# The first key tile's ten matmuls: wide part of all five slices first, the narrow part with the gate column behind them

## The chip, the cores and the metric

One core of a Trainium2 chip runs the whole kernel as one program. The metric is device time in microseconds (us).

## The reference, cut to what matters

```
g = sigmoid((x * gate_w).sum(-1, keepdims=True))     # one number for each token
a = linear attention of x (q, k, v from x @ wqkv; 32 heads of 20) @ wo
b = a two-layer mixer block on x (layernorm, w1, shift, w2, layernorm, w3, w4)
return g * a + (1 - g) * b
```

x is 2048 tokens x 640, in bfloat16. The kernel gets the gate's dot product almost for free: `gate_w` is one more column beside the 640 key columns, so the key matmul of a token tile yields 640 key columns, two columns of ones (a row sum for the layernorm) and the gate column, 643 in all. The kernel gives a matmul at most 512 columns, so a slice of the contraction (128 of 640 rows, five slices) takes a wide matmul of 512 columns and a narrow one of 131, and the gate column is in the narrow one.

## The kernel before

A scheduler of the kernel's own orders the work for each engine. Each operation lists what it reads and writes, and it waits for the last writer of everything in its lists. The loads that matter come from one queue, in this order:

```python
dma_in(x_tok[:, 0, :], ...); dma_in(x_tok[:, 1, :], ...)     # two x tiles
load_wq(0)                                                   # query weights, slice 0
dma_in(x_tok[:, 2:4, :], ...)
for k in range(1, KD):
    load_wq(k)
for k in range(KD):
    dma_in(wkg[:, k, 0:D], A_wqkv[128 * k:128 * (k + 1), D:2 * D], "wk%d" % k)     # key weights
dma_in(wkg[:, :, D + 2:D + 3], gate_w.rearrange("(k p o) -> p k o", p=128, o=1), "gw", noncontig=True)
for c in range(1, NCH):
    dma_in(x_tok[:, 4 * c:4 * c + 4, :], ...)                # 640 KB each
    ...                                                      # transposes of these x tiles
```

TensorE first runs some needless matmuls to warm up, then four query tiles with their slices mixed in the order in which weights arrive (`q_four`, 40 matmuls), then the first key tile. Both the query tiles and the first key tile go through `stream`, which makes one operation of a wide and a narrow matmul:

```python
def stream(order, w, n2, done):
    ...
        def fn(e, l=l, b=b, k=k):
            e.matmul(ps[:, b, 0:512], l, w[:, k, 0:512], start=(k == 0), stop=(k == KD - 1))
            return e.matmul(ps[:, b + 1, 0:n2], l, w[:, k, 512:512 + n2], start=(k == 0), stop=(k == KD - 1))
        pe(fn, [w[:, k, 0:512 + n2], l], [ps[:, b, 0:512], ps[:, b + 1, 0:n2]], cost=272.0)
        ...

def k_first():
    stream([(0, k) for k in range(KD)], wkg, 131, k_out)
```

Because the operation's read list is `w[:, k, 0:512 + n2]`, even its wide matmul stands behind the load of the gate column. Later key tiles (`k_tile`) run five wide and then five narrow matmuls, each group as one operation.

Of the kernel before, what the change touches and what calls it, by code (L numbers as in the profile page):

```python
# [11 lines left out]
D = 640  # L12
# [5 lines left out]
KD = D // 128  # L18
# [398 lines left out]
def _build(nc, A_x, A_wqkv, A_wo, B_w1, B_w2, B_w3, B_w4, gate_w, out, dbg=None, stop=None):  # L417
# [42 lines left out]
    ps = nc.alloc_psum_tensor("ps", [128, 8, 512], F32)  # L460
# [33 lines left out]
    xT = ra.alloc("xT", [128, KD, S], BF16)  # L494
    GT = ra.alias("GT", [128, KD, D], BF16, ra.last_addr, KD * S * 2)
    wkg = ra.alloc("wkg", [128, KD, NK], BF16)
# [34 lines left out]
    def pair():  # L531
        best = None
        for k_ in range(4):
            q_ = (bank_rr[0] // 2 + k_) % 4
            tf = 0.0
            ok = True
            for b in (2 * q_, 2 * q_ + 1):
                if b in bank_pend or b in bank_hold:
                    ok = False
                lk = sch.locks.get(b)  # L540
                if lk is not None:
                    tf = max(tf, sch.ev_time.get((lk[1].sem, lk[1].val), 1e18))
            if ok and (best is None or tf < best[0]):
                best = (tf, 2 * q_)
        b = best[1]
        bank_rr[0] = b + 2
        bank_pend.update((b, b + 1))
        return b
# [36 lines left out]
    def pe(fn, reads, writes, cost=500.0):  # L585
        for w_ in writes:
            sp_, rl = sch.rects(w_)
            if sp_ == "ps":
                for (_p0, _p1, lo, hi) in rl:
                    for b in range(lo // PS_BANK, (hi - 1) // PS_BANK + 1):  # L590
                        bank_pend.discard(b)
        return sch.op("pe", fn, reads, writes, cost=cost)
# [50 lines left out]
    def activation(out_ap, in_ap, func, scale=1.0, bias=0.0, accum=None):  # L643
        rd = [in_ap] + [a for a in (scale, bias) if not isinstance(a, (int, float))]
        wr = [out_ap] + ([accum] if accum is not None else [])
        n = nfree(out_ap)
        cost = max(150.0, 100.0 + 0.833 * n + (70.0 if in_psum(in_ap) else 0.0)) + 45.0 * (len(rd) - 1)
        if accum is not None:
            cost += 91.0
        st_ = ACT_SET.get(func)  # L650
        if st_ is not None and st_ != sch.act_func:
            cost += 1290.0
            sch.act_func = st_
        if accum is not None:
            return act(lambda e: e.activation(out_ap, in_ap, func, bias=bias, scale=scale, accum_out=accum), rd, wr, cost=cost)  # L655
        return act(lambda e: e.activation(out_ap, in_ap, func, bias=bias, scale=scale), rd, wr, cost=cost)  # L656
# [96 lines left out]
    def t_x(t):  # L753
        b = bank()
        tr_group(b, [x_tok[:, t, 128 * k:128 * (k + 1)] for k in range(KD)])
        src = psb(b, 0, D).rearrange("p (k c) -> p k c", k=KD)
        dst = xT[:, :, 128 * t:128 * (t + 1)]
        copy(dve, dst, src)

    def phi(b, dst, after_exp=None):  # L760
        se = slot("E", 3)
        src = psf[:, 512 * b:512 * b + D]
        activation(Er[:, se, :], src, ACTF.Exp)
        if after_exp is not None:
            after_exp()
        ts(dve, Er[:, se, :], Er[:, se, :], 1.0, EPS_PHI, ALU.min, ALU.add)
        return stt(dst, src, 1.0 + EPS_PHI, Er[:, se, :], ALU.add, ALU.max)
# [72 lines left out]
    def warmup(cols, cyc):  # L840
        b = bank()
        steps = [512] * (cols // 512) + [128] * (cols % 512 // 128)

        def fn(e):
            ins = None
            for n in steps:
                ins = e.matmul(ps[:, b, 0:n], xn[:, 0, 0:128], xn[:, 0, 0:128].unsqueeze(1).to_broadcast([128, n // 128, 128]), start=True, stop=True)  # L847
            return ins
        pe(fn, [xn[:, 0, 0:128]], [ps[:, b, :]], cost=cols * cyc)
# [8 lines left out]
    def stream(order, w, n2, done):  # L858
        bs = {}
        for t, k in order:  # L860
            if k is None:
                if t is None:
                    warmup(256, 0.42)
                else:
                    t_x(t)
                continue
            if k == 0:
                bs[t] = pair()
                bank_hold.update((bs[t], bs[t] + 1))
            b = bs[t]  # L870
            l = xT[:, k, 128 * t:128 * (t + 1)]
# [5 lines that stand above are left out]
            if k == KD - 1:  # L877
                bank_hold.difference_update((b, b + 1))
                done(t, b)
# [6 lines left out]
    def k_out(t, b):  # L886
        k_done[t] = phi(b, pk_tok[:, t, :], lambda: activation(lr[:, t, :], ps[:, b + 1, 129:131], ACTF.Copy))
        activation(junk[:, 0, :], x_tok[:, t, :], ACTF.Square, accum=st1[:, 1, t:t + 1])

    def k_first():  # L890
        stream([(0, k) for k in range(KD)], wkg, 131, k_out)

    def addA(name, dur, fn, deps=()):
        IT.add("A", name, dur, fn, deps)
# [4 lines left out]
    addA(("warm", 1), 0.0, lambda: warmup(WARM2, 0.42))  # L899
    addA(("q", 3), 5.44, q_four)  # L900
    addA(("k", 0), 1.36, k_first)
    for i in range(1, 4):
        addA(("k", i), 1.36, lambda t=i: k_tile(t))
# [409 lines left out]
```

## Time and profile before

| | before |
|---|---|
| median of the first three runs | 260.96 us (260.87 to 261.06) |
| span of the profiled execution | 259.6 us |
| TensorE busy | 255.7 us, 99% |
| last query matmul starts | 11.31 us |
| gate column lands | 11.71 us |
| first key matmul starts | 11.80 us |

The page of the profiled execution: span, busy time by engine (of it the share of the span, and instructions), and the chain of work that ended last.

```profile
span 259.6 us, 4300 instructions
...
PE 255.7 (99%) x1690; PEld 132.2 (51%) x1690; DVE 151.7 (58%) x287; ACT 106.8 (41%) x216; POOL 92.8 (36%) x152
...
PE 97%; DMA 1%; DVE 0%; SPq 0%; issue 0%
```

TensorE (PE) is the bound: it works nearly all the time, and the chain is 97% PE. Only time in which it waits, or does needless work, can be won without taking work away. The list of waits of PE (who waited for whom, us in total, times, longest) is short:

```profile
PE ps L847 <- POOL xn L659: 1.1, 1, 1.1
PE ps L874 <- DMA wq<-in_A_wqkv_dram: 0.5, 1, 0.5
PE ps L874 <- issue: 0.3, 1, 0.3
```

The first is the start of the kernel, the second the wait for the first query weights, and the third is the first key tile. The timeline of PE there (start, duration, engine, line, operation, output and inputs, form):

```profile
11.10 0.38 PE L874 MATMUL ps<-wq,xT 128*128 128x512 bf16 x1
11.31 0.22 PE L875 MATMUL ps<-wq,xT 128*128 128x128 bf16 x1
11.80 0.38 PE L874 MATMUL ps<-wkg,xT 128*128 128x512 bf16 x1 [0.27 <-issue]
12.01 0.22 PE L875 MATMUL ps<-wkg,xT 128*128 128x131 bf16 x1
12.07 0.38 PE L874 MATMUL ps<-wkg,xT 128*128 128x512 bf16 x1
```

Read the starts, not the durations: a matmul's recorded end lies well past the start of the next one. A wide matmul follows a narrow one after 0.06 us (12.01 to 12.07), but the first key matmul follows the last query matmul after 0.49 us. So 0.43 us are lost, where the idle time in brackets says 0.27. The DMA issue table of a window around 6.9 us shows which load is late (the last key slice, then the gate column; the last number is us from issue to landing):

```profile
wkg<-in_A_wqkv_dram SPq DMA_DIRECT2D x1, 160.0 KB, 4.1
wkg<-in_gate_w_dram SPq DMA_DIRECT2D x1, 1.2 KB, 4.7
```

The gate column is issued at 6.96 us and lands at 11.71; the key slice before it landed at 10.63. (Landings to a hundredth are the semaphore updates in the trace; the table rounds.) The first key matmul starts 0.09 us after the gate column's landing. (The trace holds 640 packets of 2 bytes, one for each element of `gate_w`, moved between 9.09 and 11.38 us.)

### The profile page before, as it was taken

To read this page: it belongs to the slowest core of one execution; us is meant where nothing else is said; L and a number is where in the kernel's file an instruction comes from. 1 tells how busy PE (TensorE), PEld (TensorE's weight loads), DVE (VectorE), ACT (ScalarE), POOL (GpSimd) and SP (SyncE) were. 2 spreads that over 40 slices of the span, in tenths; PEclk is the share of its full clock that TensorE was granted. 3 is DMA by queue.
4 is the path that set the end of the run, shared out by engine and by line. 5 is a ranking of instruction groups with operands and counts; after the bars stand their busy time and mean duration, and the time that the engine had idled before them with its cause. 6 is when DMAs were issued, how large, how long until landed. Compare 5 with 4: busy or idle time off the path is not lost.

```text
span 259.6 us, 4300 instructions
## 1 busy us (share of the span) xinstructions
PE 255.7 (99%) x1690; PEld 132.2 (51%) x1690; DVE 151.7 (58%) x287; ACT 106.8 (41%) x216; POOL 92.8 (36%) x152
## 2 busy tenths in 40 slices
PE   7999999999999999999999999999999999999996
PEld 4555555554445454554444545554455544456453
DVE  1587887899902799999998407993033410143233
ACT  1496677751355766685854240005500045200000
POOL 4003995969863019667903202230011110021001
PEclk9999999999999999999999999999999999999999
DMA  6845969572656991752726650232000020000211
GB/s 195 260 104 146 198 176 143 167 139 44 110 108 123 352 337 36 72 101 52 105 56 124 124 61 0 41 85 78 0 3 0 3 101 0 0 3 1 104 51 51
DMA packets 51348, 24.99 MB, mean 96 GB/s; under 512 B 42708, under 2 KB 49917, under 8 KB 51328
## 3 DMA queue, kind: packets, MB, share of 16 engines
q1 hardware_dynamic: 49952, 21.31, 35.2%
q0 software_dynamic: 1136, 3.28, 5.8%
q8 instruction: 13, 0.21, 0.4%
q10 hardware_dynamic: 240, 0.13, 0.2%
q14 instruction: 7, 0.06, 0.1%
HBM read 12.05 MB, written 2.62 MB: 57 GB/s over the span
## 4 chain that ended last, share of the span: by engine, by line
PE 97%; DMA 1%; DVE 0%; SPq 0%; issue 0%
PE ps L600 61%; PE ps L1152 22%; PE ps L782 8%; PE ps L874 2%; DMA wq<-in_A_wqkv_dram 1%; PE ps L1064 1%; PE ps L1134 1%; PE ps L875 1%; DVE x_tok L639 0%; PE ps L954 0%; PE ps L983 0%; SPq L285 0%; PE ps L611 0%; PE ps L1131 0%; PE ps L847 0%
## 5 line engine op out<-in xcount | busy, mean ns | idle before, releaser
L600 PE MATMUL ps<-xnT,w 128*128 128x512 bf16 x360 | 81.5, 379 | 0.0
L1152 PE MATMUL ps<-w,h2T 128*128 128x512 bf16 (+1 forms) x416 | 58.8, 299 | 0.0
L656 ACT ACTIVATE h2T<-ps 128x512 bf16<-128x512 f32 x52 | 30.5, 598 | 67.5 <-PE ps L600 67.5
L600 PEld LDWEIGHTS ps<-xnT,w 128*128 128x128 bf16 x360 | 34.2, 98 | 38.5 <-issue 0.9
L639 DVE SCALAR_TENSOR_TENSOR x_tok<-ps,stg,abx 128x512 bf16<-128x512 f32 (+1 forms) x32 | 17.3, 550 | 61.5 <-PE ps L1152 61.5
L622 POOL TENSOR_SCALAR abx<-x_tok,stg 128x640 f32<-128x640 bf16 x16 | 14.8, 927 | 99.9 <-DVE x_tok L639 94.9
L1152 PEld LDWEIGHTS ps<-w,h2T 128*128 128x128 bf16 x416 | 32.2, 98 | 24.9 <-issue 1.1
L622 POOL TENSOR_SCALAR xn<-x_tok,st 128x640 bf16<-128x640 bf16 x32 | 34.4, 1082 | 14.3 <-DMA xnT<-xn 13.6
L656 ACT ACTIVATE Er<-ps 128x640 bf16<-128x640 f32 x32 | 22.5, 705 | 17.9 <-PE ps L600 8.5
L655 ACT ACTIVATE junk<-x_tok 128x640 bf16<-128x640 bf16 x32 | 23.6, 737 | 3.1 <-DVE x_tok L637 2.6
L600 PE MATMUL ps<-M_sb,pqnT 128*128 128x512 bf16 (+1 forms) x160 | 24.3, 299 | 0.0
L656 ACT ACTIVATE hsT<-ps 128x512 bf16<-128x512 f32 (+1 forms) x32 | 18.9, 594 | 13.0 <-PE ps L600 12.6
L600 PE MATMUL ps<-w,hsT 128*128 128x512 bf16 (+1 forms) x160 | 23.7, 299 | 0.0
L600 PE MATMUL ps<-wkg,xT 128*128 128x512 bf16 (+1 forms) x150 | 22.6, 299 | 0.0
L639 DVE SCALAR_TENSOR_TENSOR abx<-ps,stg,abx 128x640 f32<-128x640 f32 x16 | 14.1, 884 | 12.7 <-PE ps L600 11.7
L600 PEld LDWEIGHTS ps<-w,hsT 128*128 128x128 bf16 x160 | 13.3, 98 | 12.2
L600 PEld LDWEIGHTS ps<-M_sb,pqnT 128*128 128x128 bf16 x160 | 13.2, 98 | 10.9
L600 PE MATMUL ps<-wq,xT 128*128 128x512 bf16 (+1 forms) x120 | 18.3, 299 | 0.0
L782 PE MATMUL ps<-pk_tok,x_tok 128*128 128x512 bf16 x80 | 17.8, 379 | 0.0
L622 DVE TENSOR_SCALAR Er<-Er 128x640 bf16<-128x640 bf16 x32 | 11.6, 363 | 9.6 <-ACT Er L656 9.2
L637 DVE SCALAR_TENSOR_TENSOR x_tok<-ps,x_tok 128x640 bf16<-128x640 f32 x16 | 13.1, 820 | 6.4 <-PE ps L600 5.9
L600 PEld LDWEIGHTS ps<-wkg,xT 128*128 128x128 bf16 x150 | 12.2, 98 | 9.0
(75 smaller groups left out, 231.2 us busy)
## 6 DMA issues: line engine op xcount, KB each, us to landing
w<-in_B_w_dram SPq DMA_DIRECT2D x1, 2160.0 KB, 9.6
w<-in_B_w_dram SPq DMA_DIRECT2D x1, 2080.0 KB, 15.2
x_tok<-in_A_x_dram SPq DMA_DIRECT2D x3, 640.0 KB, 5.9
out_dram<-x_tok SPq DMA_DIRECT2D x3, 640.0 KB, 3.1
w<-in_B_w_dram POOLq DMA_DIRECT2D x8, 160.0 KB, 4.5
wq<-in_A_wqkv_dram SPq DMA_DIRECT2D x5, 160.0 KB, 3.6
wkg<-in_A_wqkv_dram SPq DMA_DIRECT2D x5, 160.0 KB, 4.3
wv<-in_A_wqkv_dram POOLq DMA_DIRECT2D x1, 800.0 KB, 5.9
```

The lines of the kernel that those rows point to most:

```text
L600: ins = e.matmul(out_ap, l, r, start=(i == 0), stop=(i == n - 1))
L622: return engf(lambda e: e.tensor_scalar(out_ap, in_ap, s1, s2, op0, op1), rd, [out_ap], cost=cost)
L637: return dve(lambda e: e.scalar_tensor_tensor(out_ap, in0, scalar, in1, op0, op1, accum_out=accum), rd, [out_ap, accum], cost=cost + 70.0)
L639: return dve(lambda e: e.scalar_tensor_tensor(out_ap, in0, scalar, in1, op0, op1), rd, [out_ap], cost=cost)
L655: return act(lambda e: e.activation(out_ap, in_ap, func, bias=bias, scale=scale, accum_out=accum), rd, wr, cost=cost)
L656: return act(lambda e: e.activation(out_ap, in_ap, func, bias=bias, scale=scale), rd, wr, cost=cost)
L782: ins = e.matmul(o, l, r, start=(t0 + q_ == 0), stop=(t0 + q_ == NT - 1))
L874: e.matmul(ps[:, b, 0:512], l, w[:, k, 0:512], start=(k == 0), stop=(k == KD - 1))
L875: return e.matmul(ps[:, b + 1, 0:n2], l, w[:, k, 512:512 + n2], start=(k == 0), stop=(k == KD - 1))
L1064: ins = e.matmul(o, l, r, start=st, stop=sp)
L1134: ins = e.matmul(ps[:, bm, :], l, w4[rows, KFF, 0:512], start=True, stop=False)
L1152: ins = e.matmul(o, l, r, start=False, stop=(i == KFF - 1), skip_group_check=(n0 > 0))
```

## The change

It takes the wide matmuls of the first key tile out of the gate column's wait: each matmul becomes an operation that lists only its own columns, and the five wide ones come first.

```diff
     def k_first():
-        stream([(0, k) for k in range(KD)], wkg, 131, k_out)
+        b = pair()
+        for n0, n1 in ((0, 512), (512, D + 3)):
+            o = ps[:, b + n0 // 512, 0:n1 - n0]
+            for k in range(KD):
+                l, r = xT[:, k, 0:128], wkg[:, k, n0:n1]
+                pe(lambda e, o=o, l=l, r=r, k=k: e.matmul(o, l, r, start=(k == 0), stop=(k == KD - 1)), [l, r], [o],
+                   cost=(n1 - n0) * 0.4167 + 2.5)
+        k_out(0, b)
```

## The prediction

> **What bounds the kernel now.** TensorE. The page's busy table gives PE 255.7 of 259.6 us (99%), and the chain that ended last is 97% PE. The list of waits names only three waits of PE: 1.1 us for the first memset, 0.5 us for the first query weights, and 0.3 us at the first key tile, marked "issue".
>
> **The first key tile.** In the timeline the last query matmul (128 wide) starts at 11.31 us and the first key matmul at 11.80, while elsewhere in that stage a wide matmul starts 0.05 to 0.06 us after a narrow one. So PE loses 0.49 - 0.06 = 0.43 us there (the profile shows 0.27 us of idle, as a matmul's modelled end lies past the next one's start).
>
> What ends the wait: the key weights' five loads land by about 10.6 us (in the DMA issue table, 4.1 to 4.3 us each), but the gate column, 1.2 KB, is issued at 6.96 and needs 4.7 us: it lands at about 11.7, just before the PE goes on. "DMA: Bandwidth & Descriptors" in the Trainium skill (section "Rules for kernel authors") says a non-contiguous last dimension is lowered to one descriptor per element; 4.7 us for 1.2 KB, the longest of this tile's six loads, agrees. Each slice's operation reads wide and narrow columns together, so even the first wide matmul waits for the gate column, which only the narrow part uses.
>
> **What the change does.** The same ten matmuls, five wide then five narrow; nothing removed. The wide ones no longer wait for the gate column. Their other inputs are ready: weights at 10.6 us, the PSUM pair when the DVE ends query tile 0 at 11.04 (10.22 + 0.82). Five wide ones take 5 x 0.216 = 1.08 us, so the narrow part begins at about 12.45, some 0.7 us after the gate column lands: the wait vanishes. Later key tiles have this very order and take 1.36 us per ten (20 in 2.73 us in the chain), the same as five pairs at 0.27. Semaphore increments go from 5 to 10; I expect nothing from that.
>
> **How much is critical.** All of it, if what follows keeps up. The matmuls run without a visible gap from 11.80 us to the end, so all shift by 0.43 us. Nearest dangers: DVE is busy without a break from 10.2 to 16.7 us, so PSUM pairs come free at unchanged times; but the second key tile's is free at 12.13 and wanted at 12.73, the third's at 13.23 against 14.1. The first transposed x tile of the next chunk lands at about 15.9, needed at 16.84. Later handoffs hang on PE's own progress. The instruction order is made by a list scheduler from modelled costs; this tile's moves by some 5 ns, so I expect the same order.
>
> **Predicted time.** 260.96 - 0.43 = 260.53 us, 8 in 10 between 260.25 and 260.9. Chances: faster by over 2% 0.5%, within 2% 98.5%, slower by over 2% 1%.
>
> **What would show each step.** First key matmul at about 11.37; no PE wait there in the list of waits; wide starts 0.216 apart; first narrow one at about 12.45; second key tile at about 12.73 instead of 13.17; exponential of key tile 0 at about 12.94 instead of 13.37; every later stage 0.43 us earlier; span about 259.2.
>
> **What would make it wrong.** The gate column landing at another time in unprofiled runs (earlier: less gain); a reordering by the scheduler later on; a fixed-time DMA that turns the lead into a new wait; noise of 0.2 us (the three runs span 260.87 to 261.06), about half the effect.

## The result, and the profile after

| first comparison, six runs each | before | changed |
|---|---|---|
| median | 260.91 us (260.47 to 261.39) | 260.60 us (260.43 to 261.00) |
| span of the profiled execution | 259.6 us | 259.5 us |

The ratio is 0.9989, with a 95% interval of 0.9976 to 1.0002. A ratio here is the mean time of one kernel's fast runs over the mean of the other's fast runs of the same rounds, so it is not quite the ratio of the medians. The time lies in the predicted range, 0.07 us from the predicted value. But the interval includes 1, and the profile does not show 0.43 us: the span fell by 0.1 us. The page of the changed kernel:

```profile
span 259.5 us, 4269 instructions
...
PE 254.6 (98%) x1659; PEld 133.0 (51%) x1690; DVE 151.7 (58%) x287; ACT 106.7 (41%) x216; POOL 92.8 (36%) x152
...
PE 95%; DVE 2%; issue 1%; ACT 0%; POOL 0%; POOLq 0%
```

PE seems 1.1 us less busy, but its count is 1659 where there are 1690 weight loads: 31 matmul records are missing from this trace. That is not the change's doing, as later traces of the kernel before lack some too. The list of waits of PE:

```profile
PE ps L847 <- POOL xn L659: 1.1, 1, 1.1
PE ps L600 <- issue: 0.2, 1, 0.2
PE ps L1159 <- issue: 0.2, 1, 0.2
```

The wait at the first key tile is gone. The two new lines of 0.2 us are holes left by missing records: counted from the start of the second key tile, the trace of the kernel before has a matmul at each of these two places, and this trace has none. The 2% of DVE in the chain comes from such a hole too, at 16.06 us, from which the chain was followed into DVE. The timeline of PE at the first key tile:

```profile
11.48 0.38 PE L874 MATMUL ps<-wq,xT 128*128 128x512 bf16 x1
11.69 0.22 PE L875 MATMUL ps<-wq,xT 128*128 128x128 bf16 x1
11.75 1.53 PE L896 MATMUL ps<-wkg,xT 128*128 128x512 bf16 x10
13.11 0.38 PE L600 MATMUL ps<-wkg,xT 128*128 128x512 bf16 x1
```

The first key matmul now follows the last query matmul after 0.06 us, and the ten take 1.37 us, as before (by the unrounded starts 1.366 and 1.373). The mechanism works as predicted. But the last query matmul starts at 11.69 us and not at 11.31. The query stage, which the change does not touch, ended 0.38 us later in this execution. The first half of that stage in the timeline of the kernel before:

```profile
3.69 0.75 PE L611 MATMUL ps<-ident,x_tok 128*128 128x128 bf16 x10
...
5.06 0.39 PE L874 MATMUL ps<-wq,xT 128*128 128x512 bf16 x1 [0.51 <-DMA wq<-in_A_wqkv_dram]
...
5.46 0.38 PE L874 MATMUL ps<-wq,xT 128*128 128x512 bf16 x1
...
6.48 0.38 PE L874 MATMUL ps<-wq,xT 128*128 128x512 bf16 x1
```

and of the changed kernel:

```profile
3.69 1.27 PE L611 MATMUL ps<-ident,x_tok 128*128 128x128 bf16 x10
...
5.11 0.58 PE L874 MATMUL ps<-wq,xT 128*128 128x512 bf16 x1
...
5.81 0.60 PE L874 MATMUL ps<-wq,xT 128*128 128x512 bf16 x1
...
6.86 0.38 PE L874 MATMUL ps<-wq,xT 128*128 128x512 bf16 x1
```

The same instructions take longer: ten transposes 1.27 us and not 0.75, a wide matmul 0.58 to 0.60 and not 0.38, until about 6.2 us. TensorE still ran at a slow starting clock there, about half of the later one (the transposes start 0.107 us apart and not 0.056), while in the first trace it had sped up by 3.7 us (its file records full clock from 3.74 us on; the changed kernel's file has no record of the clock). The Trainium skill, "TensorE: Matmul & The Clock Gate", part "The HAM clock gate (the "warmup" mystery)", says that full clock is granted after about 3.4 us of activity measured in a free-running window, so the moment varies from run to run. That the moment varies these traces show, with a spread of more than 2 us. The 3.4 us they do not show: in the first trace full clock came 2.7 us after the first matmul (1.05 to 3.74 us).

### The profile page after: what moved, and what is told of

It reads as the page before. It is cut to its first block, busy times and chain, and to the rows that moved or that the text cites. A ratio compares the mean times of both kernels' runs of the same rounds, so it can differ in the third digit from the quotient of the medians.

```text
span 259.5 us, 4269 instructions
## 1 busy us (share of the span) xinstructions
PE 254.6 (98%) x1659; PEld 133.0 (51%) x1690; DVE 151.7 (58%) x287; ACT 106.7 (41%) x216; POOL 92.8 (36%) x152
## 4 chain that ended last, share of the span: by engine, by line
PE 95%; DVE 2%; issue 1%; ACT 0%; POOL 0%; POOLq 0%
PE ps L600 60%; PE ps L1159 21%; PE ps L782 8%; PE ps L847 1%; DVE pq_tok L639 1%; PE ps L874 1%; PE ps L1071 1%; PE ps L1141 1%; DVE Er L622 1%; PE ps L611 1%; DVE x_tok L639 0%; PE ps L961 0%; PE ps L990 0%; PE ps L875 0%; ACT Er L656 0%
## 5 line engine op out<-in xcount | busy, mean ns | idle before, releaser
L600 PE MATMUL ps<-xnT,w 128*128 128x512 bf16 x349 | 80.4, 379 | 0.6 <-issue 0.2
L600 PE MATMUL ps<-M_sb,pqnT 128*128 128x128 bf16 (+1 forms) x156 | 23.6, 297 | 0.3
```

What stands on the lines that cost most here:

```text
L600: ins = e.matmul(out_ap, l, r, start=(i == 0), stop=(i == n - 1))
```

## The experiments

The model that I tested, called A2 in the expectations, is this:

- In the kernel before, the first key matmul starts at the later of two times: the end of the query stage (last query start + 0.055 us) and the gate column's landing + 0.09 us.
- In the changed kernel, it starts at the end of the query stage.
- All that follows takes a fixed time.

The last point was read from the traces: the span less the start of the second key tile is 246.41 or 246.42 us in every trace but two (the two are told of below). So the change is worth the wait in the execution at hand, and nothing where there is none. The rivals are B (no effect, all chance) and B' (wide-then-narrow order is itself cheaper than pairs).

In all kernels below the scheduler made the same order of work as in the kernel before, and all gave correct results. "Before" is the kernel before, run on the same chip: 260.87 us for the first four, 260.86 for the next four, 260.76 for the last four.

### The changed kernel again

Edit: none.

> The changed kernel again, unedited, to narrow the interval. Theory A (the change takes away the wait for the gate column's landing): 0.2 to 0.45 us faster than before, ratio about 0.9987, the first key matmul starts 0.06 us after the last query matmul. Theory B (the change does nothing, the difference of 0.3 us so far is noise of the start): ratio 1.0000 within 0.0005.

Measured: 260.86 us, ratio 1.0003 (0.9991 to 1.0015). In its trace the last query matmul starts at 11.74 us and the first key matmul at 11.79, 0.05 us later; the gate column had landed at 11.57. So the old order would not have waited in this execution (11.57 + 0.09 is before 11.79). The size expected by A is missed, and B's ratio is met. The timeline of PE and the gate column's line of the DMA issue table (window around 6.9 us):

```profile
11.74 0.22 PE L875 MATMUL ps<-wq,xT 128*128 128x128 bf16 x1
11.79 1.53 PE L896 MATMUL ps<-wkg,xT 128*128 128x512 bf16 x10
wkg<-in_gate_w_dram SPq DMA_DIRECT2D x1, 1.2 KB, 4.6
```

In this one execution there was nothing to remove.

### The gate column's load earlier

```diff
+    dma_in(wkg[:, :, D + 2:D + 3], gate_w..., "gw", noncontig=True)
     for k in range(KD):
         dma_in(wkg[:, k, 0:D], ..., "wk%d" % k)
-    dma_in(wkg[:, :, D + 2:D + 3], gate_w..., "gw", noncontig=True)
```

> The kernel before, its matmul order untouched, with the gate column's load issued ahead of the five key loads and not behind them. Theory A (wait for the gate column): the column lands at about 9 us, before the last query matmul, the first key pair starts 0.06 us after it, and the time falls as in the changed kernel, 0.2 to 0.45 us; the key loads land 0.5 us later each, still in time. Theory B' (wide-then-narrow order itself is cheaper than pairs on TensorE): no gain, as the pairs stay.

Measured: 261.07 us, ratio 1.0008 (0.9996 to 1.0020). The column landed at 8.88 us, and the first key pair started 0.05 us after the last query matmul, so the wait was gone with pairs as well. But that query stage ended late too (last start 11.78), because the first query weights landed at 5.50 us, 0.48 later than in the first trace of before. The expected gain is missed. An execution that would not have waited gains nothing from a column that comes earlier.

### The order without the release

```diff
-    ..., [l, r], [o], cost=...)
+    ..., [l, wkg[:, k, 0:D + 3]], [o], cost=...)
```

> The changed order, five wide and then five narrow, but each wide matmul declared to read the gate column too, so that the first one waits for it as before. Theory A: same time as before within 0.1 us, the first key matmul starts about 0.09 us after the gate column lands. Theory B' (the order is what is cheaper): as fast as the changed kernel, 0.2 to 0.45 us under before.

Measured: 260.89 us against 260.87 by medians; the ratio of 1.0022 (0.9993 to 1.0051) is drawn up by two runs over 262 us. The timeline of PE:

```profile
11.48 0.22 PE L875 MATMUL ps<-wq,xT 128*128 128x128 bf16 x1
11.65 1.53 PE L896 MATMUL ps<-wkg,xT 128*128 128x512 bf16 x10
```

The first key matmul starts 0.17 us after the last query matmul and 0.09 us after the gate column's landing at 11.56, so it waited 0.12 us though it stood in the new order. The ten take 1.36 us (the second key tile starts at 13.01), within 0.02 us of the pairs. That speaks against B': the order is worth nothing in itself; it only lets the wide matmuls go ahead.

### Pairs with separate waits

```diff
+        b = pair()
+        for k in range(KD):
+            for n0, n1 in ((0, 512), (512, D + 3)):
+                ...one operation for each matmul, with the read list of its own columns
```

> Pairs kept, wide then narrow for each slice, but each matmul is an operation of its own with its own waits, so only the first narrow matmul waits for the gate column. Theory A: one wide matmul, 0.216 us, is hidden in the wait; gain 0.2 us at most, about half of the change's, and the remaining wait stands between the first wide and the first narrow matmul. Theory B' (order): no gain. A theory that ten semaphore updates in place of five cost time would show as slower than theory A by the cost.

Measured: 260.63 us, ratio 0.9995 (0.9983 to 1.0007): no gain clear of noise. In its trace the last query matmul starts at 11.54, the first wide key matmul at 11.59, the first narrow one at 11.81, and the gate column lands at 11.66. The wait would have been 0.16 us (11.66 + 0.09 - 11.59), and one wide matmul of 0.216 us covers it. Ten operations took 1.38 us (11.59 to 12.97), so ten semaphore updates in place of five cost at most 0.02 us.

### The wait made long: the gate column's load behind 640 KB of x

```diff
-    dma_in(wkg[:, :, D + 2:D + 3], gate_w..., "gw", noncontig=True)
     for c in range(1, NCH):
         dma_in(x_tok[:, 4 * c:4 * c + 4, :], ..., "xc%d" % c)
+        if c == 1:
+            dma_in(wkg[:, :, D + 2:D + 3], gate_w..., "gw", noncontig=True)
```

In the kernel before (sent twice, as no chip ran it the first time; so with the three after it):

> The kernel before with the gate column's load issued one place later, behind the 640 KB load of x. Theory A2 (before: the key tile starts at the later of query end and gate landing plus 0.09 us; change: at query end; all that follows takes 246.4 us): the column lands at about 13.4 to 14 us, the key tile starts 0.09 us after it, and the time rises by 1.6 to 2.2 us over before. Theory B (noise): the traces so far are chance and the load's place does not matter: no change.

In the changed kernel:

> The changed kernel with the gate column's load behind the 640 KB load of x. Theory A2: the five wide matmuls, 1.08 us, run inside the wait, the first narrow one starts 0.09 us after the landing; so 1.08 us faster than the same delay in the kernel before, and 0.5 to 1.1 us slower than the kernel before without the delay. Theory B' (order is what matters) and B (noise): the same as the delayed kernel before within 0.3 us.

Measured: 262.66 us (ratio 1.0075, 1.0053 to 1.0097) and 261.49 us (1.0019, 1.0004 to 1.0035). Both agree with A2, and this pair is clear of noise: the intervals of the two do not touch, and the medians are 1.17 us apart. The timeline of PE in the kernel before with the late load:

```profile
11.54 0.22 PE L876 MATMUL ps<-wq,xT 128*128 128x128 bf16 x1
13.68 0.38 PE L875 MATMUL ps<-wkg,xT 128*128 128x512 bf16 x1 [1.91 <-issue]
```

and in the changed kernel with the late load:

```profile
11.61 0.22 PE L876 MATMUL ps<-wq,xT 128*128 128x128 bf16 x1
11.66 1.24 PE L897 MATMUL ps<-wkg,xT 128*128 128x512 bf16 x5
13.63 0.46 PE L897 MATMUL ps<-wkg,xT 128*128 128x131 bf16 x5 [0.73 <-DMA wkg<-in_gate_w_dram]
13.93 0.38 PE L600 MATMUL ps<-wkg,xT 128*128 128x512 bf16 x1
```

The column landed at 13.58 and 13.59 us. Before, all ten matmuls come after it and the second key tile starts at 15.05; changed, only the five narrow ones do, and it starts at 13.93. The difference of 1.12 us is the five wide matmuls (expected: 1.08) and 0.04 us more: the first narrow matmul started 0.05 us after the landing and not the expected 0.09. (One of the six runs of the kernel before with the late load took 264.31 us at a granted clock of 0.994. By estimate, the clock lost, 0.6% of 262.7 us, is about the 1.6 us by which it lies above the median; without it the ratio of the means would be 1.0065.) This shows the mechanism: the change hides up to 1.08 us of wait for the gate column. It also shows who is being waited for, as moving nothing but that load moved the start of the key tile by 1.9 us.

### The wait taken away: a longer query stage

```diff
         def fn(e, l=l, b=b, k=k, t=t):
+            if w is wq and t == 3 and k == 0:
+                for _ in range(2):
+                    e.matmul(ps[:, b, 0:512], l, w[:, k, 0:512], start=True, stop=True)
             e.matmul(ps[:, b, 0:512], ...)
```

In the kernel before:

> The kernel before with two needless 512-wide matmuls (0.43 us) put into the query stage, their result overwritten. Theory A2: the query stage now ends at 11.7 to 12.2 us, nearly always after the gate column lands; the pad fills the wait, where there is one, so the time rises by less than 0.43 us, by about 0.25 on average, and the trace shows little or no wait at the first key tile. If the kernel before never waits: 0.43 us slower.

In the changed kernel:

> The changed kernel with the same pad. Theory A2: 0.43 us slower than the changed kernel, and the same time as the padded kernel before within 0.15 us, as with a query stage this late there is no wait left for the change to remove.

Measured: 261.37 us (1.0024, 1.0006 to 1.0041) and 261.28 us (1.0015, 0.9996 to 1.0033). The two padded kernels are 0.09 us apart, as A2 expects where no wait is left; a change without any effect (B) would show the same, so this pair does not tell the two apart. But the pad cost the kernel before 0.51 us by medians, about its full length, where I had expected 0.25: by this, the runs of before hardly waited at all. The intervals are too wide (0.9 us) to tell 0.43 from 0.25 with certainty. The trace of the padded kernel before is one of the two in which the later part was not 246.41 us: PE waited 0.8 us for a transposed x tile, which the load and transposes of x delayed.

### The kernel before against itself

> The kernel before, unedited, against itself: what the comparison makes of no change at all, and a second trace of its first key tile. Ratio 1.000 within 0.001. Theory A2: in its trace the first key matmul starts at the later of query end (last query matmul plus 0.055 us) and gate landing plus 0.09 us; the wait is between 0 and 0.45 us and differs from the 0.43 of the first trace.

Measured: 261.15 us against 260.76, ratio 1.0010 (0.9991 to 1.0029): the same kernel differs from itself by 0.39 us in its medians, more than the first gain seen for the change. The timeline of PE:

```profile
5.67 0.39 PE L874 MATMUL ps<-wq,xT 128*128 128x512 bf16 x1 [0.94 <-DMA wq<-in_A_wqkv_dram]
...
11.87 0.22 PE L875 MATMUL ps<-wq,xT 128*128 128x128 bf16 x1
11.92 0.38 PE L874 MATMUL ps<-wkg,xT 128*128 128x512 bf16 x1
```

and the DMA issue table of the window around 6.9 us:

```profile
wkg<-in_gate_w_dram SPq DMA_DIRECT2D x1, 1.2 KB, 4.1
```

The unchanged kernel does not wait for the gate column here. It waited at the start of the query stage instead, 0.94 us for the first query weights and not 0.51, and the gate column landed at 11.09, before the query stage was done. A lucky early start makes the wait at the key tile; a late one hides it.

### The changed kernel, third comparison

Edit: none.

> The changed kernel, unedited, a third comparison. Theory A2: the mean gain is the mean of the wait over executions, 0.1 to 0.25 us by the traces so far, ratio 0.9990 to 0.9997; its trace shows the first key matmul 0.05 to 0.06 us after the last query matmul.

Measured: 260.73 us against 260.76 by medians; ratio 1.0006 (0.9977 to 1.0035), with one run of 262.88 in it. The ratio misses the expected band. In its trace the last query matmul starts at 11.39 us and the first key matmul at 11.44; the column landed at 11.43, so the old order would have waited until 11.52: 0.08 us saved. The span of this trace is 259.2, the span that I had predicted, in an execution with an early query stage.

### An earlier start of the query stage

```diff
-    dma_in(x_tok[:, 1, :], x2[128:256, :], "x1")
     load_wq(0)
+    dma_in(x_tok[:, 1, :], x2[128:256, :], "x1")
```

In the kernel before, and in the changed kernel as a candidate to beat both:

> The kernel before with the first query weights' load issued ahead of the second x tile's, so that the query stage does not wait for it. Theory A2: the first query weights land about 0.3 us earlier, the query stage ends at 11.3 to 11.6 us, but the key tile still waits for the gate column until 11.6 to 12.0: gain under 0.1 us.

> The changed kernel with the same earlier load; a candidate to beat both. Theory A2: the key tile follows the query stage at once, so all that the query stage gains shows in the time: 0 to 0.2 us under the changed kernel, 0.1 to 0.4 under before, and 0.1 to 0.4 us under the same load order in the kernel before.

Measured: 261.77 us (1.0032, 1.0006 to 1.0059) and 261.38 us (1.0025, 0.9993 to 1.0056). Both expectations are missed; the idea failed. The first query weights landed at 3.6 us, but the second x tile, moved behind them, was now late: in the two traces PE waited 0.7 and 0.5 us for it. In the trace with the kernel before the slow clock lasted until 8.6 us and the last query matmul started at 13.25. In the trace with the changed kernel something else stands out in the list of waits of PE:

```profile
PE ps L600 <- DMA xT<-x_tok: 2.3, 1, 2.3
```

One DMA transpose of an x tile was issued at 37.69 us and landed only at 47.06, and TensorE stood still for it. This is the second of the two traces with a longer later part. The wait of 0.8 us in the padded kernel before was for the same transpose (issued at 38.54 us, landed at 46.40); in the first trace of before it was issued at 35.98 and landed at 41.17, and PE did not wait. Both are traces of runs above 262 us (263.17 and 262.49 us). But the trace of the kernel before with this edit is of such a run too (262.34 us), and it has no such wait; there the late end of the query stage makes up the time. So the runs above 262 us have more than one cause, and how often each comes stays open.

## Why the prediction was right or wrong

The time (260.60 measured, 260.53 predicted) and the class "within 2%" were right. This says little for the size of the effect: the predicted range reached up to 260.9 us, and three of the five medians of the unchanged kernel (260.76, 260.86 and 260.87) lie in it. Point by point:

- TensorE is the bound, and what comes after the first key tile shifts as a whole: right. The rest takes 246.41 us in the traces of both kernels.
- The gate column's landing ends the wait: right. The late load moved the key tile's start by 1.9 us, and the order with the old read lists still waited. Only the sign that was taken for one descriptor per element, the 4.7 us to landing, was weak: in the second trace of before the column took 4.1 us, less than each of the 160 KB key slices (4.2 to 4.3). The 640 packets of 2 bytes show it directly.
- The order itself costs nothing: right. Ten matmuls took 1.37 us either way, within 0.02 us. The starts 0.216 us apart agree with the formula N/2.4 + 2.5 ns of the Trainium skill, "TensorE: Matmul & The Clock Gate", section "Back-to-back issue gap". They do not agree with the 131 ns that the same section gives as a sustained figure for 512 columns.
- "260.96 - 0.43": this is the term that was mis-sized. The 0.43 us were the wait in one profiled execution. I took it off a median of other executions as though query end and gate landing stood still. Both move. Here are seven traces with query stage and load order as in the kernel before:

| trace | key tile could start (query end) | gate landing + 0.09 | wait for the column, had or spared |
|---|---|---|---|
| before | 11.37 | 11.80 | 0.43 |
| before, again | 11.92 | 11.18 | 0 |
| order without the release | 11.53 | 11.65 | 0.12 |
| pairs with separate waits | 11.59 | 11.75 | 0.16 |
| changed | 11.75 | 11.99 | 0.24 |
| changed, again | 11.79 | 11.66 | 0 |
| changed, third | 11.44 | 11.52 | 0.08 |

Where the wait is worked out rather than seen (the last column of all but the first three rows), it is the difference of the two columns, or 0. The mean is 0.15 us, an estimate of what the change is worth on average: one third of what I had put down. Even this may be high, as the first trace is the one in which the wait was found and for which the change was made; without it the mean of the other six is 0.10 us. The timed runs can't tell this from nothing: the changed kernel's median over 17 runs is 260.80 us, and that of the 28 runs of before beside them is 260.87 (by means the two are 0.02 us apart). With ratios of 0.9989, 1.0003 and 1.0006, and 1.0010 for the kernel before against itself, a gain of this size is not shown by the times. It is shown by the traces, and in the large only by the pair with the late load.

- "First key matmul at about 11.37" was therefore wrong in the traces of the changed kernel: 11.75, 11.79 and 11.44. "Exponential of key tile 0 at about 12.94" was 13.31 in the first of them.
- Among what could make it wrong I had named the gate column's landing. I had not named the more movable of the two times, the end of the query stage. Two causes of its movement are visible: the clock, slow until about 6.2 us in the first trace of the changed kernel, and the first query weights, which landed between 4.75 and 5.79 us in traces with the same load order. The seven traces tell them apart. From the first query matmul to the last it took 6.20 to 6.27 us in four of them (before; before, again; order without the release; changed, third), which began it at 5.06 to 5.67 us. It took 6.58 and 6.63 us in "changed" and "changed, again", where the slow clock lasted until about 6.2 and 5.8 us. The seventh, "pairs with separate waits", took 6.39 us and shows a third cause: PE waited 0.16 us for an x tile at 6.14 us.

So the first comparison's 0.3 us was partly luck of the draw. The change is sound, costs nothing, and makes the key tile independent of a load that lands close to its start, by up to 1.08 us.

## What to carry to other kernels

A wait that is seen in one trace is the difference of two arrival times, and the gain from removing it is the mean of that difference where it is positive, not its value in that trace. So take several traces before sizing an early, load-bound stage. Let each matmul wait for its own columns only, and put first those whose data is there. Where an effect is smaller than the noise, enlarge the suspected wait in both kernels: here that turned 0.15 us into 1.1.

## What the Trainium skill lacked or had wrong

- "TensorE: Matmul & The Clock Gate" gives the start of full clock as varying by 500 ns from run to run, though it also tells of 6, 11 or 14 slow matmuls in runs of one kernel. Here the slow clock ended near 3.7 us in one trace, near 6.2 in another and at 8.6 in a third (that one with a wait of 0.7 us between its first transposes), so the spread was far wider than 500 ns. In two traces of the changed kernel it made the query stage 0.3 to 0.4 us longer than in the first trace, about as much as the wait in question.
- The same page, "Back-to-back issue gap", calls 131 ns for 512 columns the sustained spacing and says that N/2.4 + 2.5 counts too much there. In this long run of weight load and matmul pairs the spacing was 215 or 216 ns behind 964 of the 1029 wide matmuls after 6.5 us in the first trace, as the formula says.
- No page that I read gives the spread of one load's landing time. The same 160 KB load, issued at 1.71 us, landed between 4.75 and 5.79 us in different executions; the 1.2 KB gate column, issued at 6.96 or 6.97, landed between 11.09 and 11.90.
